# Moving evictions, state reloads and the last turnings between engines in a kernel that runs a state space model and a local attention side by side

## The chip, the cores and the metric

The kernel runs on one core of one Trainium2 chip. The metric is the device time of one execution in microseconds (us). The profile of one execution comes with it, taken by the hardware profiler. Engines are named as the profile names them: PE is TensorE's matmul stream and PEld its weight loads, DVE is VectorE, ACT is ScalarE, POOL is GpSimd, SP is SyncE, which issues nearly all DMAs.

## The reference

Two independent layers over a sequence of 2048 tokens, 448 wide, in bfloat16. Their outputs are put side by side.

```python
# A: state space model, 448 complex states
Lam_bar = exp(exp(log_dt) * Lam);  B_bar = ((Lam_bar - 1) / Lam)[:, None] * Bmat
h[t] = Lam_bar * h[t-1] + B_bar @ x[t]
a[t] = 2 * real(Cmat @ h[t]) + Dskip * x[t]
# B: local attention, 16 heads of 28, 8 keys at distances 0, 2, ..., 14
q, k, v = x @ wqkv
logits[h, s, w] = dot(q[h, s], k[h, s - 2*w]) * 28**-0.5   (-1e9 ahead of token 0)
o[h, s] = sum_w softmax(logits)[h, s, w] * v[h, s - 2*w]
b = concat_heads(o) @ wo
out = concatenate([a, b], axis=-1)
```

## The kernel before

Each of the 128 partitions (chunks) holds 16 consecutive tokens, so "token j" is the j-th token of every chunk. TensorE, VectorE and ScalarE work on both layers in turn.

**Order.** The program is a list of 685 units of work, each a function that issues a few instructions. `Planner.run` (L133) walks a table of numbers, `ORDER` (L51): the number modulo 1000 is the unit, the thousands choose the engine where a unit may run on more than one. So the table sets the order in which every engine gets its instructions, and every engine works strictly in that order.

**Layer B, scores.** x arrives by DMA with its columns on the partitions. `prep` (L416) and `bank` multiply it with the weights into PSUM tiles `qk_ps` (L481, L488 for the last 64 columns), and an eviction copies each tile to SBUF: L218 and L220 are ScalarE's copy, L222 is VectorE's. VectorE multiplies q with k for each distance (`prod`, L654 for half width, L656 for full width, L660 for first sums), TensorE sums over a head's columns into `logits`. This is done for b=1 (tokens 8 to 15) first, then b=0. `softmax` (L695): TensorE adds the mask (L290), VectorE takes the maximum (L701), ScalarE the exponential (L711), VectorE normalizes (L720, L722), and a DMA on SyncE's queue turns the result (L727, `attn`).

**Layer B, values.** `v_proj` (L736) fills `vd`, with rows from the chunk before copied by DMA (`halo`). `pv` (L786) works on groups of four tokens, group 3 first, group 0 last: for each, VectorE makes four products of attention weights and values, 3584 columns each (L819), and adds them up (L822, L838). Group 0's last add is split in two halves (L841): tokens 0 and 1, then 2 and 3. Groups 3 to 1 are turned by DMA (L869). Group 0 is turned by TensorE: `tr` (L878) multiplies a token's 448 columns, taken as 4 blocks of 128, with the identity into `pt_o` (L884); 4 x 128 is 512, so the last block runs 64 columns into the next token. A copy by ScalarE, `mm` (L915, or L903 to L908 for the other groups), a copy to SBUF and a DMA follow. `wo_p` holds the rows of wo in 8 blocks of 128: block 3 and block 4 have one zero half, and blocks 4 to 7 hold the same rows as 0 to 3, shifted by 64; `swap` (L409) makes them by DMA.

**Layer A.** The parameters are worked out by `u4` (L1072) and `u6` (L1120) on GpSimd, with ScalarE's exponential and sine (L1101) between. `powers` (L1190) builds, on VectorE, the matrices of powers of Lam_bar for one of seven blocks of 64 states, m0 to m6, in a pool of four buffers `pw`. `scan` (L1206) is a chain for each block: TensorE multiplies x with `Bcat` (L1247), ScalarE evicts partial states, TensorE multiplies them with powers (L1266, L1301), and so on, each step waiting for the last. In a late step a state that lies in SBUF is put back into PSUM by a matmul with the identity (`back1` L1320, `back` L1338, matmul L1340), more products are added to it, and ScalarE evicts it (L1330, L1364). There are 16 such reloads. `outputs` (L1443) multiplies the states with `Ccat` (y, L1462), token by token. The x times Dskip of tokens 12 to 15 is made by VectorE (L1439).

`ADD`, `EADD` and `NC` are switches for steps done by a GpSimd DMA; all are zero or unused in effect.

Of the kernel before, what the change touches and what calls it, by code (L numbers as in the profile page):

```python
# [25 lines left out]
W = 8  # L26
# [13 lines left out]
NC = 3  # L40
# [6 lines left out]
ADD = (0, 0, 0, 0, 0, 0, 0)  # L47
EADD = (0, 0, 0, 0)
# [51 lines left out]
def vec2(n):  # L100
    return n / 1920.0 + 0.07
# [219 lines left out]
class PartB:  # L321
# [464 lines left out]
    def pv(self, b, prio, deps):  # L786
# [13 lines left out]
        lasts, halves, trs = {}, {}, {}  # L800
        for r in (1, 0):
            last = getattr(self, "pv_last", None)
            half = getattr(self, "u_half", None)
            ahead = half is not None
            us = (5, 4, 1, 0)
            for n in range(4):

                def step(n=n, r=r, part=0, half=half):
# [14 lines left out]
                    if n == 0:  # L823
                        mul(1 if half else 0)
                        mul(2 if half else 1)
                    elif n == 1 and half:
                        mul(3)
                        mul(0)
                    elif n == 2 and half:
                        add(1)  # L830
                        add(2)
                    elif n < 3:
                        mul(n + 1)
                        add(n)
                    elif 2 * b + r > 0:
                        add(3)
                        if not EADD[2 * b + r]:
                            V.tensor_tensor(acc[:, n1:2 * n1], acc[:, 0:n1], acc[:, n1:2 * n1], op=ALU.add)  # L838
                    else:
                        a, t = (v.rearrange("p (y j c) -> p y j c", y=2, j=4)[:, :, 2 * part:2 * part + 2] for v in (acc, tmp[3]))  # L840
                        V.tensor_tensor(a, a, t, op=ALU.add)  # L841
                dd = []
                for u in us[:2 + ahead] if n == 0 else us[n + 1 + ahead:n + 2 + ahead] if n < 3 else ():
# [3 lines left out]
                cost = 2 * vec2(2 * n1) if n < 3 else vec2(2 * n1) + vec2(n1) * (not EADD[2 * b + r]) if 2 * b + r > 0 else vec2(n1)  # L847
                last = P.add("DVE", cost, step, dd + [self.u_attn[b], last, *self.u_prod[0], *self.u_prod[1], *self.u_lg[0], *self.u_lg[1],
                                         *self.u_vm, *self.u_proj, *deps, half if n == 1 else None], prio - 0.1 * r)
# [5 lines left out]
            g = 2 * b + r  # L855
            halves[g] = self.u_half = None
            if EADD[g]:

                def merge(g=g):
                    acc = self.acc[g]  # L860
                    nc.gpsimd.dma_start(acc[:, n1:2 * n1], acc[:, 0:n1], accum_op=ALU.add)
                halves[g] = self.u_half = P.add("POOL", 1.1, merge, [last], PRI["wo"], lat=3.5)
            if not hasattr(self, "u_first"):
                self.u_first = last
        for r in (1, 0):
            g = 2 * b + r
            if g > 0:
# [5 lines left out]
                trs[r] = P.add("SP", 1.7, trd, [halves[g] or lasts[r][1]], PRI["wo"], lat=3.6)  # L873
        for j in range(j0, j0 + JB):
# [28 lines left out]
            def mm(j=j, jb=jb, g=g, e=e):  # L903
# [10 lines left out]
                for kt in range(KT):  # L914
                    nc.tensor.matmul(ps[:], lhsT=o[:, kt, :], rhs=self.wo_p[:, kt, :],  # L915
# [28 lines left out]
class PartA:  # L944
# [83 lines left out]
    def setup(self):  # L1028
# [43 lines left out]
        def u4():  # L1072
            lre, lim = o["pf"][:, 0], o["pf"][:, 1]
            dt = sm("dt")
            G.tensor_copy(dt[:], o["dt_bf"][:])
            arg = sm("arg")
            G.tensor_tensor(arg[:], dt[:], lre, op=ALU.mult)
            th = sm("th")
            G.tensor_tensor(th[:], dt[:], lim, op=ALU.mult)
            o["karg"] = karg = sm("karg", big)  # L1080
            G.tensor_tensor(karg[:], o["kv"][:], arg[:].unsqueeze(2).to_broadcast(list(big)), op=ALU.mult)
            ang = sm("ang", big)
            G.tensor_tensor(ang[:], o["kv"][:], th[:].unsqueeze(2).to_broadcast(list(big)), op=ALU.mult)
# [7 lines left out]
            G.tensor_scalar(kc[:], kf[:], C1, None, op0=ALU.mult)  # L1091
            G.tensor_tensor(angr[:], ang[:], kc[:], op=ALU.subtract)
            G.tensor_scalar(kc[:], kf[:], C2, None, op0=ALU.mult)
            G.tensor_tensor(angr[:], angr[:], kc[:], op=ALU.subtract)
# [25 lines left out]
        def u6():  # L1120
# [3 lines left out]
            G.tensor_tensor(cs[:], sh[:], sh[:], op=ALU.mult)  # L1124
            G.tensor_scalar(cs[:], cs[:], -2.0, 1.0, op0=ALU.mult, op1=ALU.add)
            la = sm("la", (NCH, 2, NM))
            G.tensor_tensor(la[:], cs[:, :, :, 0], ex[:, :, 0].unsqueeze(1).to_broadcast([NCH, 2, NM]), op=ALU.mult)
            for h in range(2):
                G.tensor_scalar(la[:, h], la[:, h], sg[:, 2 * h:2 * h + 1], sg[:, 2 * h + 1:2 * h + 2], op0=ALU.mult, op1=ALU.add)
# [469 lines left out]
```

## Time and profile before

| | |
|---|---|
| time, median of 3 runs | 139.94 us (139.92 to 139.99) |
| profiled execution | 140.0 us |
| its span | 138.3 us |
| TensorE clock granted | 0.997 |
| PE busy | 131.3 us, 95% |
| DVE busy | 123.0 us, 89% |
| ACT busy | 88.3 us, 64% |
| POOL busy | 17.7 us, 13% |
| DMA moved | 16.58 MB |

How to read the rows that follow. A row of the timeline has the start (us from the span's start), the duration, the engine, the line, the operation, out<-in, the shape, and the number of equal instructions joined in it; in brackets how long the engine was idle ahead of it and what ended that. A row of the groups has, behind the bar, the busy time in us and the mean ns of one instruction, then the idle time of the engine just ahead of them. A row of the stretches has start:end, length, then for PE, PEld, DVE, ACT, POOL the busy us with the number of instructions, the granted clock, the share of DMA and GB/s. A row of the DMA issues names the tiles, the queue, the count, the size of each, and the median us from issue to landing.

### The profile page before, as it was taken

The numbers are of one execution on the slowest core, as the hardware profiler recorded it, in microseconds if no ns is written. First come the engines' busy times: TensorE is split into PE (matmuls) and PEld (weight loads), VectorE is DVE, ScalarE is ACT, GpSimd is POOL, SyncE is SP. The second block draws the span as 40 slices with busy tenths as digits, with TensorE's granted clock in tenths as the row PEclk, the third lists the DMA queues.
The fourth block names the chain that finished last, engine by engine and source line by source line (L and its number), as shares of the span: only waits on it lengthen the run. The fifth ranks groups of instructions, "written<-read, shape, count | busy, mean of one in ns | idle before, by whom it ended". The sixth has DMA issues, their size and how long they took to land.

```text
span 138.3 us, 2835 instructions
## 1 busy us (share of the span) xinstructions
PE 131.3 (95%) x1065; PEld 67.2 (49%) x1071; DVE 123.0 (89%) x134; ACT 88.3 (64%) x199; POOL 17.7 (13%) x69
## 2 busy tenths in 40 slices
PE   7999989999999999999999999999999999999790
PEld 2534334444455453656534563556565455445450
DVE  1369998899999999997999999999999999999920
ACT  3555587998554976657695998689547151721571
POOL 7589830025000000000000000000000000000000
PEclk9999999999999999999999999999999999999998
DMA  4968965658658525648899039350093425575163
GB/s 128 269 126 208 179 87 61 153 130 95 81 113 53 97 52 112 179 104 131 167 222 198 0 67 240 95 111 0 0 95 103 139 78 118 141 163 169 35 197 100
DMA packets 41694, 16.58 MB, mean 120 GB/s; under 512 B 33685, under 2 KB 41044, under 8 KB 41681
## 3 DMA queue, kind: packets, MB, share of 16 engines
q1 hardware_dynamic: 41618, 16.40, 57.6%
q8 instruction: 8, 0.13, 0.4%
q14 instruction: 5, 0.04, 0.1%
q10 hardware_dynamic: 63, 0.01, 0.0%
HBM read 4.32 MB, written 3.67 MB: 58 GB/s over the span
## 4 chain that ended last, share of the span: by engine, by line
DVE 39%; PE 38%; SPq 9%; issue 5%; ACT 3%; DMA 3%; DVEq 0%; ACTq 0%
DVE rb L822 11%; DVE prods L819 11%; SPq L366 6%; PE v_ps L760 6%; PE scb L1247 5%; DVE rb L819 4%; PE scp L1247 4%; PE logits L672 3%; DMA rb<-in_B_x_dram 3%; DVE pw L1197 2%; PE qk_ps L481 2%; DVE prods L656 2%; PE wo_ps L915 2%; DVE rb L838 2%; ACT qk L218 1%
## 5 line engine op out<-in xcount | busy, mean ns | idle before, releaser
L819 DVE TENSOR_TENSOR prods<-attn,vd 128x3584 bf16<-128x3584 bf16 x12 | 24.0, 2018 | 0.0
L822 DVE TENSOR_TENSOR rb<-rb,prods 128x3584 bf16<-128x3584 bf16 x11 | 22.2, 2019 | 0.1
L656 DVE TENSOR_TENSOR prods<-qk 128x3072 bf16<-128x3072 bf16 (+1 forms) x15 | 19.1, 1325 | 0.0
L481 PE MATMUL qk_ps<-rb 128*128 128x512 bf16 x60 | 14.4, 379 | 0.7 <-DMA rb<-in_B_x_dram 0.6
L1462 PE MATMUL y_ps<-Ccat,qk 128*128 128x448 bf16 x60 | 14.6, 352 | 0.0
L218 ACT CAST vd<-v_ps 128x448 bf16<-128x448 f32 x16 | 7.9, 540 | 5.2 <-PE v_ps L760 4.9
L1247 PEld LDWEIGHTS <-Bcat 128*128 128x128 bf16 x84 | 7.5, 100 | 7.4 <-issue 1.1
L1294 ACT CAST ubuf<-scb 128x64 bf16<-128x64 f32 x35 | 7.3, 220 | 5.9 <-PE scb L1301 3.5
L218 ACT CAST qk<-wo_ps 128x448 bf16<-128x448 f32 (+1 forms) x16 | 8.1, 529 | 4.5 <-PE wo_ps L908 2.8
L1462 PE MATMUL y_ps<-Ccat,h 128*128 128x448 bf16 x45 | 11.0, 353 | 0.0
L1247 PE MATMUL scb<-xaT_sb,Bcat 128*128 128x512 bf16 x42 | 10.9, 380 | 0.0
L218 ACT CAST qk<-y_ps 128x448 bf16<-128x448 f32 (+1 forms) x9 | 5.6, 663 | 8.2 <-issue 4.2
L760 PE MATMUL v_ps<-rb 128*128 128x448 bf16 x48 | 10.1, 353 | 0.0
L220 ACT ACTIVATE qk<-qk_ps 64x512 bf16<-64x512 f32 (+1 forms) x15 | 8.9, 599 | 1.7 <-PE qk_ps L488 1.3
L481 PEld LDWEIGHTS <-rb 128*128 128x128 bf16 x60 | 5.6, 98 | 7.8 <-issue 1.0
L660 DVE TENSOR_TENSOR prods<-qk 128x768 bf16<-128x768 bf16 (+3 forms) x18 | 9.1, 566 | 0.1
L1462 PEld LDWEIGHTS <-qk 128*128 128x128 bf16 x60 | 5.8, 98 | 5.3 <-ACT qk L1364 0.2
L819 DVE TENSOR_TENSOR rb<-attn,vd 128x3584 bf16<-128x3584 bf16 x4 | 8.1, 2021 | 0.1
L908 PE MATMUL wo_ps<-wo_p,rb 128*128 128x448 bf16 x36 | 8.1, 353 | 0.0
L1197 DVE TENSOR_TENSOR pw<-Dm,spair 128x1920 bf16<-128x1920 bf16 x7 | 8.1, 1150 | 0.0
L218 ACT CAST qk<-qk_ps 128x512 bf16<-128x512 f32 (+2 forms) x11 | 6.3, 585 | 2.5 <-PE qk_ps L488 1.1
L1247 PE MATMUL scp<-xaT_sb,Bcat 128*128 128x512 bf16 x30 | 7.8, 381 | 0.0
(197 smaller groups left out, 259.0 us busy)
## 6 DMA issues: line engine op xcount, KB each, us to landing
out_dram<-qk SPq DMA_DIRECT2D x32, 112.0 KB, 1.8
vd<-vd SPq DMA_DIRECT2D x3, 392.0 KB, 4.5
rb<-in_B_wqkv_dram SPq DMA_DIRECT2D x3, 336.0 KB, 4.5
qk<-in_A_x_dram SPq DMA_DIRECT2D x1, 448.0 KB
ra<-in_A_B_re_dram SPq DMA_DIRECT2D x1, 392.0 KB, 4.3
ra<-in_A_B_im_dram SPq DMA_DIRECT2D x1, 392.0 KB
rb<-in_A_C_re_dram SPq DMA_DIRECT2D x4, 98.0 KB, 2.9
rb<-in_A_C_im_dram SPq DMA_DIRECT2D x4, 98.0 KB, 3.5
```

What stands on the lines that cost most here:

```text
L218: nc.scalar.copy(out, in_)
L220: nc.scalar.mul(out, in_, scale)
L366: nc.sync.dma_start(self.xT[:, j], bass.AP(x.tensor, x.offset + j * D - DT, [[T * D, NCH], [1, KT * NCH]]), transpose=True)
L481: nc.tensor.matmul(out(n), lhsT=w(n, full, k), rhs=self.xT[:, j:j + 4, k, :], start=(not rfirst and k == 1), stop=(rfirst and k == KT - 1) ...
L656: V.tensor_tensor(out.rearrange("p i j k q -> p i (j k) q"), qq.unsqueeze(1).to_broadcast([NCH, 2, 4 * nk, NCH]), bass.AP(kk.tensor, kk.of ...
L660: V.tensor_tensor(jk(out[:, i, a:e]), qq, kk, op=ALU.mult)
L760: nc.tensor.matmul(box["ps"][:].rearrange("p h d -> p (h d)"), lhsT=self.xT[:, j, k, :], rhs=self.wv[:, k, :], start=False, stop=(k == KT ...
L819: V.tensor_tensor(tmp[i].rearrange("p (j d h) -> p j d h", j=8, d=DH), aa, self.vd[:, o:o + 8], op=ALU.mult)
L822: V.tensor_tensor(acc, acc, tmp[i], op=ALU.add)
L1197: V.tensor_tensor(t[:], self.o["Dm"][:].rearrange("p (a b) -> p a b", b=2).unsqueeze(1).to_broadcast([NCH, 2 * NPW, 32, 2]), self.sp[:, m ...
L1247: mt(box[i], lhsT=self.Bcat[:, k, m, :], rhs=self.xk(slice(i, None, 4), k), start=(i % 2 == 0 and k == 0), stop=False, **kw)
L1462: nc.tensor.matmul(ps, lhsT=h, rhs=self.Ccat[:, m, :], start=(m == 0 and not skip), stop=(m == NM - 1), skip_group_check=True)
```

## The change

The 685 units stay the same ones. What they do or where they stand changes:

- `ADD`, `EADD`, `NC` and the code behind them go.
- `u4` and `u6` may run on VectorE or GpSimd; the table leaves both on GpSimd. GpSimd's masks move behind `u6`.
- The pool `pw` has five buffers, so block m's powers wait for the end of block m-5, not m-4.
- A reload may be made by ScalarE, which copies the state into PSUM. The table chooses this for 7 of the 16: two of m0, three of m2, one of m4, one of m5.
- Tokens 1 and 3 of group 0 are read 64 columns to the left: token 1's four blocks start in the last 64 columns of token 0 and end with token 1. The projection takes the shifted blocks 4 to 7 of `wo_p`, whose block 4 has zeros for the foreign half.
- Evictions of q and k change engines: nine go from VectorE to ScalarE, four the other way; one of Bcat and a few SBUF copies change too.
- The table is another one throughout. VectorE has five of the seven power builds ahead of the value products instead of four. On SyncE's queue the load of wo moves ahead of Dskip's, two halo copies of v move forward, the last two move behind the turnings of the softmax. Token 15's y product moves from ahead of group 0's turnings to between the projections of tokens 2 and 3; token 7's and the projections of tokens 7 and 11 move ahead of group 0's turnings.

```diff
-ADD = (0, 0, 0, 0, 0, 0, 0)
-EADD = (0, 0, 0, 0)
...
-    28, 45, 1043, 49, 50, 67, 62, 63, 44, 1042, 30, 1068, 51, 64, 54, 21, 29, 31, 35, 32, 220, 1052, 1066, 55,
+    1, 22, 4, 5, 2, 3, 0, 36, 7, 38, 39, 24, 1037, 26, 28, 30, 8, 6, 40, 9, 41, 42, 19, 13, 12, 49, 1043, 11,
...
             def tr(j=j, jb=jb):
                 pt = jb["pt"] = self.psum.tile([NCH, KT, NCH], f32, name="pt_o", tag="s")
-                a = j % 4 * D
+                a = j % 4 * D - 64 * (j % 2)
...
-                    nc.tensor.matmul(ps[:], lhsT=o[:, kt, :], rhs=self.wo_p[:, kt, :],
+                    nc.tensor.matmul(ps[:], lhsT=o[:, kt, :], rhs=self.wo_p[:, 4 * (j % 2) + kt, :],
...
-        a4 = P.add("POOL", 4.3, u4, [a3, cx.boot], -5)
+        a4 = P.add(("POOL", "DVE"), (4.3, 2.3), u4, [a3, cx.boot], -5, until=0.0)
...
-            t = pool.tile([NCH, 2 * NPW, 32, 2], bf16, name="pw", tag="pw", bufs=4)
+            t = pool.tile([NCH, 2 * NPW, 32, 2], bf16, name="pw", tag="pw", bufs=5)
...
-            pwb, u_pw = self.powers(m, -3 if m < 2 else PRI["pw"] + m * 0.1, [done[m - 4]] if m > 3 else [])
+            pwb, u_pw = self.powers(m, -3 if m < 2 else PRI["pw"] + m * 0.1, [done[m - 5]] if m > 4 else [])
...
+            def reload(eng, out, e):
+                if eng == "ACT":
+                    nc.scalar.copy(out, e)
+                else:
+                    mt(out, lhsT=cx.ident[:], rhs=e, start=True, stop=False, **kw)
+
+            def back1(eng, box=box, reload=reload):
                 t = self.psum.tile([NCH, 512], f32, name="scb1", tag="s")
                 box[1] = t[:]
-                mt(box[1], lhsT=cx.ident[:], rhs=box["e1"][:], start=True, stop=False, **kw)
+                reload(eng, box[1], box["e1"][:])
...
+            def back(n, eng, box=box, pair=pair, hget=hget, reload=reload):
...
-                mt(box[2 * n], lhsT=cx.ident[:], rhs=hget()[:, 2 * n, :], start=True, stop=False, **kw)
...
+                reload(eng, box[2 * n], hget()[:, 2 * n, :])
```

In the rows of the issue order, `qk_ps` is a PSUM tile of q or k, `prods` a product of q and k or of attention and values, `pw` one block's powers, `Gd` a factor of Bcat.

VectorE while the parameters and the last q and k of b=1 arrive, before:

```order
L222 CAST qk<-qk_ps 128x4x128
L654 TENSOR_TENSOR prods<-qk 128x1536 x2
L1197 TENSOR_TENSOR pw<-Dm,spair 128x1920
L1145 TENSOR_TENSOR Gd<-Dm,gs 128x896
L1197 TENSOR_TENSOR pw<-Dm,spair 128x1920
L654 TENSOR_TENSOR prods<-qk 128x1536
L579 COPY qk<-qk 64x8
L654 TENSOR_TENSOR prods<-qk 128x1536
L222 CAST qk<-qk_ps 64x4x128
L222 COPY rb<-rb 64x4x128
```

The same place after:

```order
L219 CAST qk<-qk_ps 128x4x128
L651 TENSOR_TENSOR prods<-qk 128x1536
L219 COPY rb<-rb 64x4x128
L219 COPY ra<-ra 128x7x64
L651 TENSOR_TENSOR prods<-qk 128x1536
L1127 TENSOR_TENSOR Gd<-Dm,gs 128x896
L1179 TENSOR_TENSOR pw<-Dm,spair 128x1920 x3
L219 CAST qk<-qk_ps 128x4x128
L651 TENSOR_TENSOR prods<-qk 128x1536
L219 CAST Bcat<-ps_b 128x4x128
```

Three powers follow the factor Gd in one piece, where before two powers stood around it, and an eviction of Bcat has come to VectorE.

VectorE from the first normalization of the softmax (b=1) to the first value products, before:

```order
L720 RECIPROCAL rsum<-sm_ps 128x128
L722 TENSOR_TENSOR attn_t<-ex_sb,rsum 128x1024
L660 TENSOR_TENSOR prods<-qk 128x768 x2
L660 TENSOR_TENSOR prods<-qk 128x1536
L660 TENSOR_TENSOR prods<-qk 128x768 x2
L660 TENSOR_TENSOR prods<-qk 128x1536
L701 TENSOR_REDUCE mx<-logits 128x128
L819 TENSOR_TENSOR rb<-attn_1004,vd 128x3584
```

The same place after:

```order
L717 RECIPROCAL rsum<-sm_ps 128x128
L719 TENSOR_TENSOR attn_t<-ex_sb,rsum 128x1024
L1046 CAST dsk<-pd 128x4
L1179 TENSOR_TENSOR pw<-Dm,spair 128x1920
L698 TENSOR_REDUCE mx<-logits 128x128
L1179 TENSOR_TENSOR pw<-Dm,spair 128x1920
L814 TENSOR_TENSOR rb<-attn_1132,vd 128x3584
```

The six sums of b=0's products now stand ahead of the normalization, and behind it there are two powers and Dskip's cast.

ScalarE around the first finished states of the scan (`h` and `e` are states in SBUF, `scb` and `scp` states in PSUM), before:

```order
L1307 CAST S<-scb_875 128x128
L1294 CAST ubuf_139<-scb_892 128x64
L1263 CAST h_136<-scp_997 128x512
L1263 CAST h_136<-scp_980 128x512
L1314 CAST h_134<-scb_875 128x384
L1294 CAST ubuf_139<-scb_892 128x64 x2
L1329 CAST h_134<-scb_1083 128x512
L1294 CAST ubuf_139<-scb_892 128x64
```

The same place after:

```order
L1289 CAST S<-scb_880 128x128
L1304 CAST scb_985<-e_897 128x512
L1262 CAST eA<-scb_934 128x256
L1296 CAST h_134<-scb_880 128x384
L1304 CAST scp_1002<-h_134 128x512
L1317 CAST h_134<-scb_985 128x512
L1269 CAST eB<-scb_934 128x128
L1337 CAST h_134<-scp_1000 128x512
L1337 CAST h_134<-scp_1002 128x512
```

Two copies into PSUM (L1304) have come into ScalarE's row, the first of them ahead of a step of another chain (`eA`).

More of the change, by code (lines that the diff above doesn't have):

```diff
@@ L39 @@
 NF = 3
-NC = 3
 WARM = 6
@@ L799, in pv, with step @@
         self.oTd = getattr(self, "oTd", {})
-        lasts, halves, trs = {}, {}, {}
+        lasts, trs = {}, {}
         for r in (1, 0):
             last = getattr(self, "pv_last", None)
-            half = getattr(self, "u_half", None)
-            ahead = half is not None
             us = (5, 4, 1, 0)
             for n in range(4):
-                def step(n=n, r=r, part=0, half=half):
+                def step(n=n, r=r, part=0):
                     alloc()
@@ L823, in step @@
                     if n == 0:
[L824 to L827, printed above, removed]
                         mul(0)
-                    elif n == 2 and half:
-                        add(1)
-                        add(2)
+                        mul(1)
                     elif n < 3:
@@ L836, in step @@
                         add(3)
-                        if not EADD[2 * b + r]:
-                            V.tensor_tensor(acc[:, n1:2 * n1], acc[:, 0:n1], acc[:, n1:2 * n1], op=ALU.add)
+                        V.tensor_tensor(acc[:, n1:2 * n1], acc[:, 0:n1], acc[:, n1:2 * n1], op=ALU.add)
                     else:
@@ L842, in pv @@
                 dd = []
-                for u in us[:2 + ahead] if n == 0 else us[n + 1 + ahead:n + 2 + ahead] if n < 3 else ():
+                for u in us[:2] if n == 0 else us[n + 1:n + 2] if n < 3 else ():
                     o = j0 + 4 * r + DIL * u
@@ L854, in pv @@
             self.pv_last = last
[L855 to L862, printed above, removed]
             if not hasattr(self, "u_first"):
@@ L872, in trd @@
                     nc.sync.dma_start(t, self.acc[g][:, n1:2 * n1], transpose=True)
-                trs[r] = P.add("SP", 1.7, trd, [halves[g] or lasts[r][1]], PRI["wo"], lat=3.6)
+                trs[r] = P.add("SP", 1.7, trd, [lasts[r][1]], PRI["wo"], lat=3.6)
         for j in range(j0, j0 + JB):
@@ L1090, in u4 @@
             kc = sm("kc", big)
[L1091 to L1094, printed above, removed]
+            E.tensor_scalar(kc[:], kf[:], C1, None, op0=ALU.mult)
+            E.tensor_tensor(angr[:], ang[:], kc[:], op=ALU.subtract)
+            E.tensor_scalar(kc[:], kf[:], C2, None, op0=ALU.mult)
+            E.tensor_tensor(angr[:], angr[:], kc[:], op=ALU.subtract)
         def u5():
@@ L1138, in u6 @@
             for h in range(2):
-                G.tensor_tensor(sp[:, :, h], e2, cs[:, h].rearrange("p m k -> p (m k)").unsqueeze(2).to_broadcast([NCH, n, 2]),
+                E.tensor_tensor(sp[:, :, h], e2, cs[:, h].rearrange("p m k -> p (m k)").unsqueeze(2).to_broadcast([NCH, n, 2]),
                                 op=ALU.mult)
@@ L1160, in setup @@
         a3 = P.add("ACT", 0.3, u3, [a2], -5)
-        a4 = P.add("POOL", 4.3, u4, [a3, cx.boot], -5)
+        a4 = P.add(("POOL", "DVE"), (4.3, 2.3), u4, [a3, cx.boot], -5, until=0.0)
         a4b = P.add("DVE", 1.3, u4b, [a2], -4.5)
         a5 = P.add("ACT", 2.2, u5, [a4], -5)
-        a6 = P.add("POOL", 6.0, u6, [a5, a4b], -5)
+        a6 = P.add(("POOL", "DVE"), (4.7, 2.2), u6, [a5, a4b], -5, until=0.0)
         self.u_g = P.add("DVE", vec2(896), u7, [a6], -4)
@@ L1399, in scan @@
             if not hold[2]:
-                u = P.add("PE", pe(1, 512), back1, [u], PRI["bk"] + m * 0.1, acq="s")
+                u = P.add(("PE", "ACT"), (pe(1, 512), act(512) + 0.1), back1, [u], PRI["bk"] + m * 0.1, acq="s", until=0.0)
             u = P.add("PE", pe(2, 256), s5, [u, u3], pc)
@@ L1403, in scan @@
             b0 = b2 = eh
-            add = bool(ADD[m])
-            if not hold[0] and not add:
-                b0 = P.add("PE", pe(1, 512), lambda f=back: f(0), [b0], PRI["bk"] + m * 0.1, acq="W" if pair else "s")
-            if not hold[pair ^ 1] and not add:
-                b2 = P.add("PE", pe(1, 512), lambda f=back: f(1), [b2, b0], PRI["bk"] + m * 0.1, acq=None if pair else "s")
-            v0 = P.add("PE", pe(2, 256), s6, [b0, u3], pc, acq=("W" if pair else "s", "cP") if add else None)
-            v2 = P.add("PE", pe(1, 512), s7, [b2, u1, v0 if add and pair else None], pc, acq="s" if add and not pair else None)
+            if not hold[0]:
+                b0 = P.add(("PE", "ACT"), (pe(1, 512), act(512) + 0.1), lambda e, f=back: f(0, e), [b0], PRI["bk"] + m * 0.1, acq="W" if pair else "s", until=0.0)
+            if not hold[pair ^ 1]:
+                b2 = P.add(("PE", "ACT"), (pe(1, 512), act(512) + 0.1), lambda e, f=back: f(1, e), [b2, b0], PRI["bk"] + m * 0.1, acq=None if pair else "s", until=0.0)
+            v0 = P.add("PE", pe(2, 256), s6, [b0, u3], pc)
+            v2 = P.add("PE", pe(1, 512), s7, [b2, u1], pc)
             if pair:
@@ L1415, in scan @@
             done[m] = P.add("POOL", 0.0, lambda: None, [w0, w2, u1], rel=("fl", "pw"), lat=0.0)
-            if add:
-                w0 = w2 = P.add("POOL", 1.2, addin, [w0, w2], pc, rel="cP", lat=3.0)
             self.u_h.append((w0, u1, w2, [u3, eh]))
```

72 lines of the change are left out of this document (30 added, 42 removed), and 62 rows, old and new, of the table ORDER.

## The prediction

> **What bounds the kernel now.** I read the page first: the share of each engine, then the chain that ended last.
>
> ```profile
> span 138.3 us, 2835 instructions
> PE 131.3 (95%) x1065; PEld 67.2 (49%) x1071; DVE 123.0 (89%) x134; ACT 88.3 (64%) x199; POOL 17.7 (13%) x69
> DVE 39%; PE 38%; SPq 9%; issue 5%; ACT 3%; DMA 3%; DVEq 0%; ACTq 0%
> ```
>
> TensorE and VectorE are both nearly full and share the chain; ScalarE is not. So a gain must come off both, or off the ends. Next, VectorE in order of time, at the points where the chain changes.
>
> ```profile
> 30.24 1.76 DVE L656 TENSOR_TENSOR prods<-qk 128x3072 bf16<-128x3072 bf16 x1
> 56.82 0.95 DVE L720 RECIPROCAL rsum<-sm_ps 128x128 f32<-128x128 f32 x1
> 57.87 1.23 DVE L722 TENSOR_TENSOR attn_t<-ex_sb,rsum 128x1024 bf16<-128x1024 bf16 x1
> 59.02 3.69 DVE L660 TENSOR_TENSOR prods<-qk 128x768 bf16<-128x768 bf16 x6
> 63.51 1.22 DVE L701 TENSOR_REDUCE mx<-logits 128x128 bf16<-128x1024 f32 x1 [0.80 <-PE logits L290]
> 64.65 2.02 DVE L819 TENSOR_TENSOR rb<-attn,vd 128x3584 bf16<-128x3584 bf16 x1
> 126.48 2.09 DVE L841 TENSOR_TENSOR rb<-rb,prods 128x1792 bf16<-128x1792 bf16 x2
> 128.49 1.08 DVE L1439 TENSOR_TENSOR qk<-qk,rb 128x1792 bf16<-128x1792 bf16 x1
> ```
>
> Between 30.24 and 63.51 one wait is left (0.80 us); from 64.65 VectorE multiplies and adds attention weights with values, to the two halves of the last add at 126.48. I call the end of its first half T0: 126.48 + 1.09 = 127.57. Last, TensorE at the end.
>
> ```profile
> 121.25 1.50 PE L1462 MATMUL y_ps<-Ccat,S 128*128 128x448 bf16 x7
> 127.63 0.51 PE L884 MATMUL pt_o<-ident,rb 128*128 128x128 bf16 x6
> 128.63 0.29 PE L884 MATMUL pt_o<-ident,rb 128*128 128x128 bf16 x2 [0.49 <-DVE rb L841]
> 128.76 0.73 PE L908 MATMUL wo_ps<-wo_p,rb 128*128 128x448 bf16 x3
> 131.98 0.61 PE L884 MATMUL pt_o<-ident,rb 128*128 128x128 bf16 x8 [0.17 <-DVE qk L1474]
> 132.43 2.43 PE L915 MATMUL wo_ps<-wo_p,rb 128*128 128x448 bf16 x12
> 134.94 0.53 ACT L218 CAST qk<-wo_ps 128x448 bf16<-128x448 f32 x1 [0.23 <-PE wo_ps L915]
> ```
>
> TensorE reaches the first turning (pt_o) at 127.63, just when T0 lets it; token 1's turning then stops for the second half of the add. Everything behind, to the last copy at T0 + 7.37, is a tail: turn, copy, project, copy, store.
>
> **The change part by part.**
>
> *Evictions.* Nine 512-column evictions of q, k move from VectorE to ScalarE, five (four of q, k and one of Bcat) the other way; of the SBUF copies VectorE loses two (wm and one duplicate of B's x) and gains three.
>
> ```profile
> L222 DVE CAST qk<-qk_ps 128x512 bf16<-128x512 f32 x5 | 3.3, 685 | 0.4 <-POOL kc L1093 0.3
> L222 DVE COPY rb<-rb 64x512 bf16<-64x512 bf16 x2 | 0.6, 290 | 0.1
> L654 DVE TENSOR_TENSOR prods<-qk 128x1536 bf16<-128x1536 bf16 x6 | 5.7, 956 | 1.0 <-ACT qk L218 0.9
> L1197 DVE TENSOR_TENSOR pw<-Dm,spair 128x1920 bf16<-128x1920 bf16 x7 | 8.1, 1150 | 0.0
> L1145 DVE TENSOR_TENSOR Gd<-Dm,gs 128x896 bf16<-128x896 bf16 x1 | 0.6, 615 | 0.0
> 18.34 2.75 PE L481 MATMUL qk_ps<-rb 128*128 128x512 bf16 x12 [0.56 <-DMA rb<-in_B_x_dram]
> ```
>
> That is -4 x 0.685 + 0.29 = -2.45 us of VectorE work, all ahead of 30.24. It doesn't all count: the x of tokens 4 to 7 arrives by DMA, and TensorE waits for it until 18.34; SyncE's queue up to there is unchanged. From then VectorE has, ahead of the product that starts at 30.24: two copies (0.58), four half products (3.82), Gd (0.62), three powers (3.45), four evictions (2.74), pads (about 0.4) = 11.6 us by durations, 10.4 us if each of some 15 instructions overlaps the next by 0.08 (as 63.51 + 1.22 ends 0.08 behind the start of the next row). I take 11.1, as waits undo some of the overlap: 18.4 + 11.1 = 29.5 in place of 30.24, **-0.7**. Bounds: 0, if ScalarE, which now carries these evictions, is late by as much; -2.45 if nothing waits. I take -0.7, since it is the sum of the rows.
>
> *Parameters.* Both parameter blocks may now run on VectorE, but the issue order keeps them on GpSimd: no cost, no gain. GpSimd's masks move behind them, and on ScalarE the sine moves behind three evictions (3 x 0.6). That puts the end of spair near 18.2, by the sum below of ScalarE's rows, and VectorE asks for it near 20: hidden by the products ahead.
>
> ```profile
> 9.91 0.60 PE L488 MATMUL qk_ps<-rb 64*128 64x512 bf16 x4
> ...
> 47.21 1.28 ACT L711 ACT_TABLE_LOAD   x1
> 48.51 1.02 ACT L711 ACTIVATE ex_sb<-logits 128x1024 bf16<-128x1024 f32 x1
> L218 ACT CAST qk<-qk_ps 128x512 bf16<-128x512 f32 x7 | 3.9, 589 | 1.1 <-PE qk_ps L488 1.1
> L1101 ACT ACTIVATE sh<-angr,turn 128x105 f32<-128x105 f32 x2 | 0.7, 376 | 1.3 <-POOL mrow L275 1.3
> 17.49 0.11 POOL L1212 MEMSET S<- 128x14 bf16 x1
> 12.87 0.54 POOL L1124 TENSOR_TENSOR cs<-sh 128x210 f32<-128x210 f32 x1
> ```
>
> ScalarE: the matmuls of 9.91 that finish the first q and k come some 0.8 earlier, since four others (0.22 each) move behind them, so the first eviction is ready near 9.7; 3 x 0.55 with overlap, exponent 0.3, table 1.28, two sines 0.7 = 13.6; GpSimd's block took 17.49 - 12.87 = 4.6, so 18.2. In these rows a table switch costs 1.30 us from its start to the next activation. The Trainium skill, "ScalarE: Activation LUTs", section "What ACT_TABLE_LOAD costs", adds a drain of about 1.38 us to every switch; this trace doesn't show it. By that rule the sine and all evictions behind it would be 1.4 later; it returns as a rival.
>
> *Powers, softmax and the first value product.* With five buffers for powers, five of seven builds now stand ahead of the value products, not four, and two products move ahead of the first normalization. That ends at 59.10 - 0.7 - 1.07 (one power fewer ahead; starts of consecutive rows) + 3.69 (the two products) = 61.0. Its turning by DMA took:
>
> ```profile
> 59.13 1.50 SPq L727 DMA_TRANSPOSE attn<-attn_t  x1
> DMA to landing us min/median/max: 3.1/3.1/3.1
> 63.27 0.21 PE L290 MATMUL logits<-mrow,mcol 128*128 128x4 bf16 x2
> ```
>
> so attention weights land at 61.0 + 0.03 + 3.1 = 64.1. Meanwhile VectorE does dsk 0.07, a power 1.07, the maximum 1.14, a power 1.07: until 64.4. The 0.80 us wait for the masks' matmul (63.27) goes if TensorE gets there by 62.1: the third state's x matmuls (eight slots of 0.22) now stand behind it, 63.27 - 1.8 = 61.5. Value products start at 64.4 with 1.14 us (one power, dsk) less behind them: T0 = 64.4 + (127.57 - 64.65) - 1.14 = 126.2, **-1.4 in all**, -0.7 of it from here. The next limit is that DMA, 0.3 us ahead. On SyncE's queue the third halo of v moves behind the second softmax's turning:
>
> ```profile
> vd<-vd SPq DMA_DIRECT2D x3, 392.0 KB, 4.5
> ```
>
> seven value operations of 1.94 and one of 1.09 from 64.4, a power, a normalization of 2.3, 1.5 of issue: 84.0, landed by 88.5. The fourth product of the second group needs it near 82.5 + 1.07 + 4 x 1.94 = 91.3, so 2.8 us in hand.
>
> *Seven reloads by ScalarE.* Of 16 identity matmuls that put a state back into PSUM, seven become copies.
>
> ```profile
> 67.34 0.38 PE L1340 MATMUL scp<-h,ident 128*128 128x512 bf16 x1
> 67.56 0.38 PE L1266 MATMUL scb<-h,pw 128*128 128x512 bf16 x1
> L1364 ACT CAST h<-scp 128x512 bf16<-128x512 f32 x6 | 3.4, 603 | 0.0
> 70.00:80.00 10.00, 9.76 (x72) 5.08 (x71) 9.93 (x6) 8.03 (x27) 0.00 (x0) 1.00 0.62 122
> ```
>
> TensorE issues the next matmul 0.22 after one: 7 x 0.22 = -1.5 us. No row shows ScalarE writing PSUM; the nearest, of the same size, reads PSUM in 0.60, so +4.2 us on ScalarE, which is 8.0 of 10 us busy there (ACT is the fourth busy figure). Bounds: 0 if all hide, 4.2 if each stands in the path of a scan; I take +0.2, since seven copies spread over some 40 us leave ScalarE under 9 in 10. The Trainium skill, same page, "Step-by-step: what each stage is for", calls ScalarE's writes to PSUM faster than those to SBUF; no row here shows one, and a lower price would only shorten the 4.2.
>
> TensorE must be at the turning by 126.2. Ahead of it: -1.5 (reloads), -1.34 (token 15's seven y matmuls, 121.25 to 122.59, move into the tail), +0.57 (token 7's three, now ahead): 127.63 - 2.3 = 125.3. Up to 0.9 in hand, less where waits are rearranged.
>
> *Tail.* Tokens 1 and 3 are read 64 columns earlier, so token 1 no longer touches token 2's columns: tokens 1 and 0 turn right after T0. TensorE from T0, at 0.45 per turning and 0.75 per projection (2.43 for three, less the last's overlap): two turnings to 1.0, token 2's half is added at T0 + 1.09 and turned by 1.6, three projections by 3.85, token 3's turning 4.3, y of token 15 5.65, last projection 6.4, last copy starts at T0 + 6.5. ScalarE's copies (0.6 each) hide under the projections, token 3's under y. 6.5 for 7.37: **-0.9**.
>
> Sum: 138.3 - 1.4 - 0.9 + 0.2 = 136.2. The profiled execution took 140.0 us, 1.7 more than its span, and the runs' median is 139.94; so **137.9 us**.
>
> **Rivals.** About 0.2% (0.28 us) is what a measurement of this kernel can tell from no change.
>
> *ScalarE's queue becomes the bound of the scan (slower).* Place: 56 to 98 us, where copies of two chains alternate in one queue and TensorE waits in order. If each reload holds a chain's next copy back by its 0.60 and nothing fills TensorE, T0 = 125.5 + 4.2 = 129.7, and 129.7 - 127.57 - 0.9 = +1.2: 141.2. It decides once TensorE's waits pass 3 us (T0 over 128.5). For it: 8.0 of 10 busy. Against: TensorE's waits for ScalarE in this scan are almost nil now, and independent x matmuls stand between the steps. 0.18.
>
> *TensorE only just keeps up.* Its waits eat the 1.4 and T0 stays, the tail alone gains: 139.1. 0.14.
>
> *The early stretch gives all of it.* -2.45 in place of -0.7; then TensorE's 125.3 is the limit of T0, some 125.5 with the 0.2 of waits: 140.0 - 2.1 - 0.9 = 137.0. For: VectorE lost 2.45 us of work. Against: the 18.34 of the DMA stands. 0.14.
>
> *The table switch drains.* Everything on ScalarE behind the sine 1.4 later, up to 30 us, T0 back at 127.6: 139.3. That is the page's rule; the 1.30 us of the rows speaks against it. 0.03.
>
> **How the numbers follow.** Forecast 0.47 (137.3 to 138.7); with the three faster rivals 0.78 is faster by over 0.2%. Same 0.04, for ScalarE waits that cancel the gain; slower 0.18. The range leaves out the slower case and takes in the rest, 137.0 with 0.4 below it: 136.6 to 140.0.
>
> **What would show it.** Right: the first full-size product near 29.5; no wait ahead of the maximum; first value product near 64.4; T0 near 126.2 with TensorE's pt_o waiting for VectorE; token 1's turning whole; last copy about 6.5 behind T0. Wrong: TensorE waits for ScalarE's reloads totalling over 1 us; VectorE idle for attention weights; pt_o starting well behind T0 because TensorE is late.

## The result, and the profile after

| | before | after |
|---|---|---|
| time, median of 4 runs | 139.97 us (139.92 to 140.22) | 138.92 us (138.71 to 139.07) |
| ratio to before | | 0.9921 (95% interval 0.9900 to 0.9941) |
| profiled execution, its span | 140.0, 138.3 us | 138.77, 137.1 us |

The change gains 1.05 us, about half of the 2.0 that were forecast (137.9), and inside the range. The page of after, its shares and its chain:

```profile
PE 130.2 (95%) x1059; PEld 66.2 (48%) x1064; DVE 121.8 (89%) x131; ACT 94.1 (69%) x209; POOL 20.9 (15%) x69
PE 60%; DVE 19%; SPq 10%; ACT 4%; DMA 3%; issue 2%; DVEq 0%; ACTq 0%
```

The chain that ended last was VectorE's and TensorE's in nearly equal parts (39% and 38%); now TensorE has 60% of it. VectorE's timeline at the points of the prediction:

```profile
30.34 1.76 DVE L653 TENSOR_TENSOR prods<-qk 128x3072 bf16<-128x3072 bf16 x1
60.39 1.23 DVE L719 TENSOR_TENSOR attn_t<-ex_sb,rsum 128x1024 bf16<-128x1024 bf16 x1
62.90 1.22 DVE L698 TENSOR_REDUCE mx<-logits 128x128 bf16<-128x1024 f32 x1 [0.15 <-PE logits L287]
65.33 2.03 DVE L814 TENSOR_TENSOR rb<-attn,vd 128x3584 bf16<-128x3584 bf16 x1
126.03 2.09 DVE L829 TENSOR_TENSOR rb<-rb,prods 128x1792 bf16<-128x1792 bf16 x2
```

T0, the end of the first half of the last add, is 126.03 + 1.09 = 127.12: 0.45 earlier than before, not 1.4. TensorE's timeline at the end, and ScalarE's last copy:

```profile
126.60 0.92 PE L1432 MATMUL y_ps<-Ccat,qk 128*128 128x448 bf16 x4
127.36 1.50 PE L864 MATMUL pt_o<-ident,rb 128*128 128x128 bf16 x24
128.70 2.43 PE L895 MATMUL wo_ps<-wo_p,rb 128*128 128x448 bf16 x12
130.97 0.61 PE L864 MATMUL pt_o<-ident,rb 128*128 128x128 bf16 x8
131.42 1.49 PE L1432 MATMUL y_ps<-Ccat,S 128*128 128x448 bf16 x7
132.74 0.92 PE L895 MATMUL wo_ps<-wo_p,rb 128*128 128x448 bf16 x4
133.70 0.53 ACT L215 CAST qk<-wo_ps 128x448 bf16<-128x448 f32 x1 [1.01 <-PE wo_ps L895]
```

No bracket stands behind any TensorE row: it arrives at the turning at 127.36, 0.24 after T0, and none of these rows waits. By these rows an earlier T0 would have won nothing: TensorE was the one that came late. The last copy starts at T0 + 6.58 (before: T0 + 7.37).

### The profile page after: what moved, and what is told of

It is laid out like the page before. It is cut to its first block, busy times and chain, and to the rows that moved or that the text cites. A ratio compares the mean times of both kernels' runs of the same rounds, so it can differ in the third digit from the quotient of the medians.

```text
span 137.1 us, 2829 instructions
## 1 busy us (share of the span) xinstructions
PE 130.2 (95%) x1059; PEld 66.2 (48%) x1064; DVE 121.8 (89%) x131; ACT 94.1 (69%) x209; POOL 20.9 (15%) x69
## 4 chain that ended last, share of the span: by engine, by line
PE 60%; DVE 19%; SPq 10%; ACT 4%; DMA 3%; issue 2%; DVEq 0%; ACTq 0%
PE y_ps L1432 15%; DVE prods L653 7%; SPq L363 7%; PE scb L1229 6%; PE wo_ps L888 5%; PE scp L1229 5%; DVE prods L657 3%; DMA rb<-in_B_x_dram 3%; DVE pw L1179 3%; DVE prods L651 2%; PE logits L669 2%; PE wo_ps L895 2%; PE scb L1283 2%; PE scP L1229 2%; PE v_ps L757 2%
## 5 line engine op out<-in xcount | busy, mean ns | idle before, releaser
L1229 PE MATMUL scb<-xaT_sb,Bcat 128*128 128x512 bf16 x42 | 11.1, 381 | 0.1
L217 ACT ACTIVATE qk<-qk_ps 128x512 bf16<-128x512 f32 (+1 forms) x17 | 9.8, 598 | 1.8 <-PE qk_ps L485 1.7
L1276 ACT CAST ubuf<-scb 128x64 bf16<-128x64 f32 x35 | 6.7, 217 | 3.8 <-PE scb L1283 1.8
L215 ACT CAST qk<-qk_ps 128x512 bf16<-128x512 f32 (+2 forms) x14 | 8.2, 587 | 1.3 <-POOL angr L1073 1.0
```

What stands on the lines that cost most here:

```text
L215: nc.scalar.copy(out, in_)
L217: nc.scalar.mul(out, in_, scale)
L1229: mt(box[i], lhsT=self.Bcat[:, k, m, :], rhs=self.xk(slice(i, None, 4), k), start=(i % 2 == 0 and k == 0), stop=False, **kw)
```

## Experiments

All are the changed kernel's code with the edits shown. Each result is the ratio of a kernel's time to that of before on the same chip, with its 95% interval; the change has 0.9921 (0.9900 to 0.9941). Differences between two experiments are those of their ratios, taken times 140 us. A row of numbers in a diff is a piece of `ORDER`.

### The reloads back on TensorE (e1_reload_pe)

```diff
-1250 1254 1328 1331 1332 1405 1440
+250 254 328 331 332 405 440
```

> The changed kernel with all 16 reloads back on TensorE, the rest of the table as it is. Theory A (from about 95 us on TensorE has no idle time, so it sets the end, and T0 is only 0.24 us ahead of it): TensorE gets 7 x 0.216 = 1.5 us more and reaches the turning at 128.6 to 128.9 in place of 127.36; time 140.1 to 140.4. Theory B (the reloads on ScalarE delay the scan by about what they save): 138.7 to 139.2. Theory C (VectorE's T0 sets the end): T0 stays at 127.1 and the time rises by at most 0.3.

1.0079 (1.0058 to 1.0100), slower than before. The timeline, and a row of TensorE's waits (total us, times, longest):

```profile
126.20 2.09 DVE L829 TENSOR_TENSOR rb<-rb,prods 128x1792 bf16<-128x1792 bf16 x2
129.47 1.50 PE L864 MATMUL pt_o<-ident,rb 128*128 128x128 bf16 x24
```

```profile
PE scp L1306 <- ACT qk L1296: 0.6, 1, 0.6
```

T0 stays (127.29), TensorE comes 2.1 us later: 1.5 of matmuls, and one reload waits 0.6. Theory A holds, by more than it said: in this sequence the seven reloads on ScalarE are worth 1.6%.

### Tokens 1 and 3 unshifted (e2_noshift), and the shift with the old table (e3_old_table)

```diff
-                a = j % 4 * D - 64 * (j % 2)
+                a = j % 4 * D
-                    nc.tensor.matmul(ps[:], lhsT=o[:, kt, :], rhs=self.wo_p[:, 4 * (j % 2) + kt, :],
+                    nc.tensor.matmul(ps[:], lhsT=o[:, kt, :], rhs=self.wo_p[:, kt, :],
```

> The changed kernel with tokens 1 and 3 of group 0 read unshifted again (and projected with blocks 0 to 3), the table as it is. Theory A: the turning of token 1 waits for the second half of the last add, which ends near 128.1, so TensorE stands still for 0.5 to 0.8 us; time 139.4 to 139.7. Theory B (TensorE would have waited for ScalarE's copies anyway): within 0.2 of the changed kernel, 138.8 to 139.1.

0.9934 (0.9921 to 0.9946): 0.2 us over the change, which the two intervals don't tell apart. TensorE's timeline:

```profile
127.55 1.79 PE L864 MATMUL pt_o<-ident,rb 128*128 128x128 bf16 x24
```

The size is Theory B's, but not its reason: TensorE comes to the turning at 127.55, half a microsecond ahead of the end of the second half of the add (128.10), so little of the wait is left, and the 24 matmuls of the first three turnings take 1.79 for 1.50. For e3 the code stays and `ORDER` is that of before.

> The changed kernel's code with the table of before: of the whole change only the shifted turning takes effect. Theory A: the 0.49 us that token 1's turning waited goes, and part of the waits behind it; the last copy comes 6.7 to 6.9 behind T0 in place of 7.37; time 139.4 to 139.6. Theory B (the shift is the whole of the tail's gain): 0.8 to 0.9 less, 139.1. Theory C (what follows is bound by ScalarE's copies): no change, 139.9.

0.9995 (0.9983 to 1.0007): no gain. TensorE's timeline there shows that the wait only moved:

```profile
130.45 0.92 PE L895 MATMUL wo_ps<-wo_p,rb 128*128 128x448 bf16 x4 [1.29 <-DVE qk L1444]
```

The turnings no longer wait for VectorE, but the first projection behind them does, 1.29 us, for L1444, which drains the y tiles of tokens 12 to 15 from PSUM behind the last add. Theory C's outcome, with another cause: not ScalarE's copies but PSUM tiles.

### x of tokens 4 to 7 earlier (e4_x_early)

```diff
-19, 13, 12, 49, 1043, 11, 10
+13, 12, 49, 1043, 11, 10, 19
```

(19 is the load of B; the copy of its last columns, 1154, moves behind unit 33 as well.)

> The changed kernel with the load of B (two DMAs, 1.33 us of SyncE's queue) moved behind the turned loads of x of tokens 4 to 7, and the copy of B's last columns behind the factor Gd on VectorE. Theory A (VectorE's work from 18.5 to 30.3 us hangs on the arrival of that x, and TensorE waits 1.3 us for it): the first full-size product starts at 29.1 to 29.5 in place of 30.34, T0 near 126.0, TensorE at the turning near 126.2; time 137.6 to 138.0. Theory B (ScalarE's evictions, nine more of them, bound that stretch): the product stays within 0.3 of 30.34, time 138.6 to 139.0. Theory C (the matrix Bcat comes late instead): TensorE waits at its matmuls near 22 us and the time is 139.2 or more.

0.9926 (0.9913 to 0.9938): no change. VectorE's timeline:

```profile
14.87 0.69 DVE L221 TENSOR_SCALAR qk<-qk_ps 128x512 bf16<-128x512 f32 x1 [1.11 <-PE qk_ps L511]
18.72 0.51 DVE L219 COPY rb<-rb 64x512 bf16<-64x512 bf16 x1
21.14 0.47 DVE L219 COPY ra<-ra 128x448 bf16<-128x448 bf16 x1 [0.39 <-DMA ra<-in_A_B_im_dram]
30.79 4.03 DVE L653 TENSOR_TENSOR prods<-qk 128x3072 bf16<-128x3072 bf16 x3
```

In the changed kernel the same eviction and the same copy stand at:

```profile
14.50 0.69 DVE L221 TENSOR_SCALAR qk<-qk_ps 128x512 bf16<-128x512 f32 x1 [1.11 <-PE qk_ps L511]
18.54 0.29 DVE L219 COPY rb<-rb 64x512 bf16<-64x512 bf16 x1 [0.47 <-DMA rb<-in_B_x_dram]
```

The copy at 18.72 no longer waits for x, and nothing is won: counted from that eviction of VectorE's, the product comes after 15.92 us (14.87 to 30.79), and after 15.84 in the changed kernel (14.50 to 30.34). Theory A falls as it was put. In the changed kernel's 15.84 us VectorE's rows show one wait, the 0.47 us for x, so an earlier x could win no more than that; here it is gone, and B's last columns are late by 0.39. No row there waits for ScalarE either, so Theory B has the size but not the reason. By these rows it is VectorE's own list of work from 14.50 on that sets 30.34; ahead of that VectorE waits for TensorE's q and k, in four places and for 4.0 us in all (the last are the 1.11 us). No run moves that stretch by itself.

### The evictions back on their engines (e9_evict_back)

```diff
-42 52 53 65 72 85 86 99 119 120 48  1045 1047 1154 1073 1094 1114 1102 1166
+1042 1052 1053 1065 1072 1085 1086 1099 1119 1120 1048  45 47 154 73 94 114 102 166
```

> The changed kernel with every moved eviction and copy back on the engine that it had before (11 to VectorE, 8 to ScalarE), the sequence as it is. Theory A (the 2.4 us taken from VectorE only became idle time at 10 to 18.5 us; behind that the two lists weigh the same): the first full-size product starts at 30.0 to 30.8 and the time stays within 0.3 us of the changed kernel, 0.990 to 0.9945 of before. Theory B (VectorE's 2.45 us count): the product at 31.0 or later, 0.996 to 1.006 of before.

1.0085 (1.0066 to 1.0104): Theory B's outcome, and worse than its range. VectorE's first full-size product, and two waits of TensorE:

```profile
33.05 4.03 DVE L653 TENSOR_TENSOR prods<-qk 128x3072 bf16<-128x3072 bf16 x3 [0.52 <-PE ps_b L1163]
```

```profile
PE ps_b L1163 <- ACT ra L215: 1.3, 1, 1.3
PE qk_ps L485 <- DVE rb L219: 0.8, 1, 0.8
```

The product comes 2.7 us later, and TensorE now waits for copies that stand behind evictions. But it is not VectorE's work that grew: in the first 30.3 us VectorE is busy for 20.45 us here and for 21.36 in the changed kernel. It waits for TensorE's q and k, 4.6 us in three places up to 21.1 us. So Theory B's reason doesn't show, and what the copies and what the evictions cost was not separated. The new sequence needs the new engines. The stretches of before, then of after (start:end, length, then PE, PEld and DVE busy) show what became of VectorE's time:

```profile
10.00:18.50 8.50, 7.93 (x41) 3.11 (x41) 7.94 (x14) 4.81 (x10) 7.72 (x21) 1.00 0.92 164
```

```profile
10.00:18.50 8.50, 7.27 (x35) 2.75 (x33) 5.63 (x8) 8.29 (x16) 5.09 (x11) 1.00 0.82 163
18.50:30.30 11.80, 11.71 (x106) 5.59 (x107) 11.54 (x16) 9.44 (x19) 4.91 (x7) 1.00 0.53 109
```

From 10 to 18.5 us VectorE's work falls from 7.94 to 5.63 us, and TensorE's as well, from 7.93 to 7.27; the product still comes at 30.34. What VectorE lost there is idle time, and from 18.5 to 30.3 us, where it is nearly full, it has 11.54 us of work for 10.73 before.

### Old tail in the new table (e5_old_tail), new tail in the old one (e8_new_tail)

In e5 the last 57 units stand in the sequence of before; the projections of tokens 11 and 7, and token 15's y (unit 682), are back in their places.

```diff
-586 581 591 588 583 593 597 682 599      turn 1, 0, 2; project 1, 0, 2; turn 3; y 15; project 3
+682 ... 554 586 613 591 588 597 581 593 599 583
```

> The changed kernel with its last 57 units in the sequence of before: token 15's y is again ahead of group 0's turnings and VectorE drains y of tokens 12 to 15 in one piece. Theory A (the three y tiles wait in PSUM for VectorE until 1.3 us behind T0, and TensorE, which has six such tiles, stands still for about 1.3 us, as it did with the table of before): 0.7 to 1.0 us over the changed kernel, so 0.997 to 0.9995 of before. Theory B (TensorE is full to the end, so the sequence of its work does not matter): within 0.15 us of the changed kernel, 0.991 to 0.993 of before.

1.0036 (1.0024 to 1.0048): 1.6 us over the change, Theory A's direction and more than it said.

```profile
121.82 0.73 PE L1432 MATMUL y_ps<-Ccat,h 128*128 128x448 bf16 x3 [0.99 <-ACT qk L215]
129.91 0.61 PE L864 MATMUL pt_o<-ident,rb 128*128 128x128 bf16 x8 [0.34 <-DVE qk L1444]
```

TensorE waits 1.33 us for PSUM, here mostly for ScalarE's copies of y (the 57 units took other work into their old places too), the rest for VectorE's. e8 is the converse: before's table, all reloads on TensorE, and only its last 52 units (those from unit 602 on in its table) in the sequence of after.

> The changed kernel's code with the table of before up to the projections of group 1, and from there (52 units) the sequence of the changed kernel; all reloads on TensorE. Theory A (the tail gains by itself, since TensorE at 126.8 is ahead of T0 at 127.5): the last copy 6.5 to 6.6 behind T0, 0.993 to 0.995 of before. Theory B (the tail's gain needs the lighter TensorE): TensorE reaches the turning 0.5 us or more behind T0, 0.997 to 1.000 of before.

0.9927 (0.9914 to 0.9939): not to be told from the whole change (the profiled spans are 137.5 and 137.1 us). VectorE, TensorE and ScalarE:

```profile
126.56 2.09 DVE L829 TENSOR_TENSOR rb<-rb,prods 128x1792 bf16<-128x1792 bf16 x2
127.70 1.62 PE L864 MATMUL pt_o<-ident,rb 128*128 128x128 bf16 x24 [0.72 <-DVE rb L829]
134.16 0.53 ACT L215 CAST qk<-wo_ps 128x448 bf16<-128x448 f32 x1 [1.00 <-PE wo_ps L895]
```

TensorE is ready at 126.98 and waits for T0 (127.65); the last copy starts at T0 + 6.51. Theory A.

### The new tail without the shift (e12_new_tail_noshift)

e8 with the edit of e2.

> As e8_new_tail, with tokens 1 and 3 of group 0 unshifted. Theory A (TensorE is ready before T0 there, so the turning of token 1 waits for the second half of the last add, 1.0 us behind T0): 0.5 to 1.0 us over e8_new_tail, 0.996 to 1.000 of before. Theory B (as in e2_noshift, where it cost 0.2 to 0.3): 0.994 to 0.995.

0.9992 (0.9975 to 1.0009), 0.9 us over e8 by the ratios, 0.5 by the profiled spans (138.0 and 137.5 us):

```profile
127.67 0.51 PE L864 MATMUL pt_o<-ident,rb 128*128 128x128 bf16 x6 [0.73 <-DVE rb L829]
128.67 1.18 PE L864 MATMUL pt_o<-ident,rb 128*128 128x128 bf16 x18 [0.49 <-DVE rb L829]
```

Token 1's turning stops again for the second half: Theory A. So the shift alone (e3) and the sequence of the last 52 units alone (e12) give nothing that can be measured, and both together 0.73%: each removes one of two waits that lie behind one another. Which of the moves in those 52 units does it (the later y of token 15 is one) was not separated.

### Reloads elsewhere (e6_old_table_reload, e7_reload_all, e11_late_reloads)

```diff
e6, in the table of before:   -250 254 328 331 332 405 440
                              +1250 1254 1328 1331 1332 1405 1440
e7, in the changed table:     -253 289 292 293 366 402 406 443 444
                              +1253 1289 1292 1293 1366 1402 1406 1443 1444
```

> The changed kernel's code with the table of before, and in it the same seven reloads on ScalarE (so, beside e3_old_table, the reloads alone). Theory A (with the old table VectorE's T0 of 127.5 and the PSUM tiles it drains behind it set the end): TensorE reaches the turning near 126.1 and waits there for VectorE; 0.998 to 1.000 of before. Theory B (TensorE sets the end): 1.5 us less, 0.988 to 0.990 of before. Theory C (the copies hold the scan back): 1.003 or more.

1.0428 (1.0388 to 1.0467): Theory C, far above its lower bound. TensorE's waits, and then its stretches of 2 us in one place (the granted clock stands third from the end):

```profile
PE scb L1299 <- ACT scb L1304: 2.4, 3, 1.2
PE scp L1299 <- ACT scp L1304: 2.3, 2, 1.7
PE scp L1331 <- ACT scp L1304: 1.3, 1, 1.3
```

```profile
82.00:84.00 2.00, 0.79 (x8) 0.43 (x7) 2.00 (x2) 1.48 (x5) 0.00 (x0) 1.00 1.01 191
84.00:86.00 2.00, 0.42 (x4) 0.15 (x3) 2.00 (x2) 2.00 (x5) 0.00 (x0) 0.96 1.00 169
86.00:88.00 2.00, 1.87 (x13) 1.42 (x13) 1.71 (x3) 2.00 (x7) 0.00 (x0) 0.50 0.91 326
88.00:90.00 2.00, 2.00 (x9) 0.63 (x9) 1.90 (x3) 0.75 (x2) 0.00 (x0) 0.68 0.00 0
```

Six waits, 6.0 us in all, for copies of 0.6: they stand behind other evictions in ScalarE's row. From 82 to 86 us TensorE is busy for 1.21 us of 4, and then runs at half clock.

> The changed kernel with all 16 reloads on ScalarE. Theory A (TensorE, 1.95 us lighter, is ready before T0, so VectorE's T0, 0.24 us ahead now, becomes the limit): 0.2 to 0.4 us less than the changed kernel, 0.989 to 0.991 of before. Theory B (nine more copies of 0.60, 5.4 us, overfill ScalarE at 60 to 95 us, where it is 0.87 to 0.93 busy, and TensorE waits for them): 0.995 of before or more.

1.0204 (1.0170 to 1.0238): Theory B. TensorE comes to the turning at 132.15, 4.8 us later. In five places it waits for ScalarE, 3.0 us in all, three of them for a reload; the granted clock is 0.985. The rest of the 4.8 was not followed up.

e11 builds on e10 below and puts only three on ScalarE, near 94 to 99 us.

```diff
-443 ... 444 ... 406
+1443 ... 1444 ... 1406
```

> As e10_power_in_gap, with three reloads (one of m4, two of m5, near 94 to 99 us) on ScalarE. Theory A (a reload in ScalarE's row stands ahead of evictions that TensorE waits for, and the table was not laid out for it): TensorE waits 0.3 to 0.6 us for each, 0.9 to 1.8 us less the 0.65 us of matmuls; 0.990 to 0.996 of before. Theory B (three reloads find room): 0.986 to 0.989.

1.0019 (1.0003 to 1.0035), 1.9 us over e10 and above Theory A's range; its profiled span is 1.4 over e10's.

```profile
PE scP L1331 <- ACT scP L1304: 0.6, 1, 0.6
PE scp L1331 <- ACT scp L1304: 0.5, 1, 0.5
```

Two waits make 1.1 us; the rest of the loss does not show as a wait, and was not followed up. A copy of a reload takes 0.6 us in all of these kernels; what decides is what stands ahead of it.

### A power in the gap (e10_power_in_gap)

e8, where TensorE waited for T0, leaves VectorE as the bound; the 0.80 us that it waits for the mask can hold a power.

```diff
-213, 214, ... 533, ... 373
+213, 373, 214, ... 533
```

> As e8_new_tail (table of before, sequence of the changed kernel only for the end), and block m4's powers moved from behind the first value product into VectorE's wait of 0.80 us ahead of the second maximum. Theory A (TensorE is ready at 126.98 and waits 0.7 us for T0 there, so VectorE sets the end): T0 comes 0.8 us earlier, near 126.85, the time falls by 0.6 to 0.8 us to 0.987 to 0.989 of before. Theory B (a power earlier costs VectorE or TensorE elsewhere as much): within 0.2 us of e8_new_tail, 0.991 to 0.994.

0.9886 (0.9864 to 0.9908), 138.36 us: Theory A.

```profile
62.74 1.15 DVE L1179 TENSOR_TENSOR pw<-Dm,spair 128x1920 bf16<-128x1920 bf16 x1
63.81 1.22 DVE L698 TENSOR_REDUCE mx<-logits 128x128 bf16<-128x1024 f32 x1
125.71 2.09 DVE L829 TENSOR_TENSOR rb<-rb,prods 128x1792 bf16<-128x1792 bf16 x2
126.86 1.62 PE L864 MATMUL pt_o<-ident,rb 128*128 128x128 bf16 x24
```

The maximum follows the power without a wait, T0 is 126.80, and TensorE reaches the turning just then. The move needs the fifth buffer: matmuls of m0 still read m0's powers at 64.86 us (L1331), so with four buffers m4's could not be written at 62.74. This is the fastest kernel of the study. It beats before clearly and the change by 0.35%, at which the two intervals still touch (0.9900 to 0.9941 for the change).

## Why the prediction was half right

**Evictions (-0.7, got +0.1).** This term failed: the product was to come at 29.5 and came at 30.34. 0.14 us of that is the start, 18.54 for 18.4. The rest is the sum: it allowed 11.1 us, and VectorE needed 11.8. The 0.5 us allowed for overlap was right (the durations add up to 12.3). Two things were too short. The two copies at 18.5 take 0.29 and 0.64 us, not 0.58 together. And Gd with the three powers takes 0.4 us more than in the rows of before, 0.73 and 1.25 each for 0.62 and 1.15. In the changed kernel and in e9:

```profile
20.93 3.59 DVE L1179 TENSOR_TENSOR pw<-Dm,spair 128x1920 bf16<-128x1920 bf16 x3
```

```profile
24.42 3.28 DVE L1179 TENSOR_TENSOR pw<-Dm,spair 128x1920 bf16<-128x1920 bf16 x3
```

In the changed kernel GpSimd's masks, moved behind `u6`, run from 19.4 to 23.6 us, beside these powers; in e9 they end at 18.9. "No cost, no gain" was the prediction's price for that move; the rows point to 0.4 us (see the last section), though no run moves the masks alone. The bound of 0 was the right end, but not for its reason, a late ScalarE: VectorE doesn't wait for ScalarE there.

**Powers and softmax (-0.7, got -0.55).** Right, in size and in reason. From the first full-size product to T0: 127.57 - 30.24 = 97.33 before, 127.12 - 30.34 = 96.78 after; 0.65 of it is the wait ahead of the maximum (0.80 to 0.15). The first value product came at 65.33, not 64.4, for the 0.84 of the first term and that 0.15.

**Reloads.** The price from the nearest row was right. The copies into PSUM (ns, min/median/max):

```profile
L1304 ACT CAST scb<-e x3: 589/590/597, 60.7 to 95.7; 128x512 f32<-128x512 bf16 x3
L1304 ACT CAST scp<-h x3: 612/623/624, 61.9 to 84.5; 128x512 f32<-128x512 bf16 x3
```

A copy into PSUM took 0.59 to 0.62 us, one out of it into SBUF 0.60 (the mean of L1337), and one from SBUF to SBUF 0.62 (`wm`, 128x512, bf16). The Trainium skill, "ScalarE: Activation LUTs", section "Step-by-step: what each stage is for", calls the way to PSUM the faster one; these rows don't show it. The +0.2 for the scan can't be read off a run by itself; what the reloads were worth hung on the sequence: they won 1.6% in one and cost 4.3% in another.

**TensorE at the turning (125.3, got 127.36).** The second failure, and the larger one. The 2.3 us of matmuls did leave. But the prediction carried before's waits over, and the new sequence has more. e1 and e8 have the same TensorE work; e1 reaches the turning at 129.47, e8 could at 126.98: 2.5 us. In the stretches up to 127 us TensorE is idle for 1.75 us more in e1 than in e8: 0.65 of it at 90 to 105 us, where e1's reload waits, 0.4 at 10 to 18.5, and 0.4 at 45 to 57, where a matmul of the softmax waits for VectorE's maximum. The changed kernel has that wait too, and before has none there:

```profile
PE logits L702 <- DVE mx L698: 0.6, 1, 0.6
```

Its wait for x is 1.33 us, for 0.56 before. The remaining 0.7 of the 2.5 doesn't show as idle time and stays open. "Less in hand where waits are rearranged" was said and not priced.

**Tail (T0 + 6.5, got + 6.58).** Right in size, -0.8 for -0.9, and the experiments add the cause: the shift and the new sequence of the end work only together.

**The account.** -0.45 at T0 and -0.8 in the tail make the span's -1.2. In time, the tail by itself gives 0.73% of before, the whole change 0.79%; the intervals don't tell them apart. So evictions, sequence and reloads together win nothing that can be measured: in the new sequence the reloads are worth 1.6% and the evictions with their copies 1.6%, and what is left over for the sequence by itself, as a difference (no run has it alone), is a loss of that order. The measured 138.92 is outside the forecast's own 137.3 to 138.7, and inside the range only because that took in the rivals. It lies next to the 139.1 of "TensorE only just keeps up", and most of that rival's account came true: TensorE's waits ate what it was to have in hand, and the tail gave nearly all. The slower rival did not come, but its mechanism is real: e6, e7 and e11 are slower by 1.3 to 4.3% than the kernels that they were made from.

**The table switch.** In the changed kernel:

```profile
11.35 1.28 ACT L1082 ACT_TABLE_LOAD   x1
12.65 0.66 ACT L1082 ACTIVATE sh<-angr,turn 128x105 f32<-128x105 f32 x2
```

It is 1.30 us from the start of the load to the sine. The Trainium skill, "ScalarE: Activation LUTs", section "What ACT_TABLE_LOAD costs", adds a drain of about 1.38 us; again it doesn't show, and that rival falls.

## What to carry to other kernels

When one engine's work is cut, ask where the freed time lies: of VectorE's work 2.3 us went from a stretch in which it then waits for TensorE's matmuls, and became idle time. And work on an engine with room to spare may not be free: GpSimd's masks, moved behind `u6`, ran beside VectorE's powers, and there both took longer; what causes it was not tested. Two waits that lie behind one another hide each other, so a fix that measures nothing alone may be half of one that measures; try the pair. Moving a small step to a less busy engine is priced by what stands ahead of it in that engine's row, not by the engine's share of busy time: the same seven copies gave 1.6% in one sequence and cost 4.3% in another.

## What the runs showed of the hardware

In e6, TensorE was busy for 1.21 us of the 4 from 82 to 86 us, and the granted clock then fell to 0.50 and 0.68 in the next two stretches of 2 us, in the middle of a kernel that is otherwise at 1.00. The Trainium skill, "TensorE: Matmul & The Clock Gate", section "What's actually happening", has half clock follow an idle window of about 3.4 us. The half clock agrees; but TensorE was not idle for that long at a stretch here, its longest wait is 1.71 us. The waits cost more than themselves: three matmuls of L1300 (128x384) took 0.32 to 0.33 us each ahead of 84 us, and the next, at 86.19, 0.52.

GpSimd's four selects, which make its masks, took 0.35 us each before (near 12 us) and 0.68 to 1.21 us after, beside VectorE's Gd and powers at 20 to 24 us; no wait for them shows:

```profile
L283 POOL TENSOR_SCALAR_AFFINE_SELECT mcol<-mcol x4: 347/348/359, 11.7 to 12.6; 128x128 bf16<-128x128 bf16 x4
```

```profile
L280 POOL TENSOR_SCALAR_AFFINE_SELECT mcol<-mcol x4: 682/1182/1214, 19.4 to 22.3; 128x128 bf16<-128x128 bf16 x4
```

VectorE's side shows it too. In the changed kernel, e1, e2, e5 and e7 the selects run beside Gd and the three powers, which take 0.73 and 1.25 us. In before, e9 and all runs with the sequence of before they run earlier, and Gd and the powers take 0.62 and 1.14 to 1.15. In e4 they start behind Gd and end ahead of the last power: 0.62 for Gd, then 1.20, 1.25 and 1.15. No run moves the selects alone, so that one causes the other is not proven.
